# Chunk attention with two feed-forward layers: attention scores and values of a pair of heads as one operation each, from block 2 on

## The chip, the cores and the metric

The kernel runs on one core of one Trainium2 chip. The metric is the device time of one execution in microseconds, as the median over runs. Five engines work side by side and wait for one another by semaphores: TensorE (PE, with its weight loads as PEld), VectorE (DVE), ScalarE (ACT), GpSimd (POOL) and the queue of SyncE (SP) that issues transfers.

## The reference

Chunked attention with memory, then two feed-forward layers one behind the other on its output, all in float32. Inputs: q, k, v of 4 batches x 8 heads x 768 positions x 64; 8 memory keys and values for each head; weights 512x2048 and 2048x512 for each layer.

```
for c in range(nc):                          # chunks of 32 queries
    l_start = max(0, c_start - 16)
    r_end = min(S, c_end + 8)
    k_full = concat([mem_k, k[l_start:r_end]]);  v_full likewise
    scores = scale * q_c @ k_full.T
    a = softmax(scores)
    out[c_start:c_end] = a @ v_full
x = out as 3072 tokens x 512
x = (h * tanh(softplus(h))) @ w_out          # h = x @ w_in     (layer 1)
return (h * sigmoid(1.702 * h)) @ w2_out     # h = x @ w2_in    (layer 2)
```

## The kernel before

The 3072 tokens are cut into 8 blocks of 384 (`TB`), half a batch each. For a block the program does attention over all 8 heads, which leaves the block's activations split in a high and a low part (`xh`, `xl`, 128 x 4 x 384 each, one slice of 384 for each pair of heads), and then layer 1 in 16 steps of 128 hidden units (`step`): 12 matmuls of 128x384 into a bank `h` (line 904), the activation on ACT (916), a split in `gh` and `gl`, and 12 matmuls into the four output banks `o` (line 933). Each product is taken as three matmuls on the split parts. Layer 2 (lines 1066 and 1093) follows when all blocks are through layer 1.

The attention of block j runs in the gaps of layer 1 of block j-1. Blocks 0 and 1 (`EARLY`) are done in another way and stay as they are; from block 2 on a block has 4 pairs of heads, and each pair has two **quads**. A quad is 2 groups of 96 queries x 2 heads. `quad` (line 690) makes the scores of the quad: four f32 matmuls on 64 rows of the array (one head in rows 0-63, the other in rows 64-127), 96 queries against a window of 128 keys, head 0 into bank `s0`, head 1 into bank `s1`; each f32 matmul is two MATMUL instructions in the trace. Then DVE adds the mask and takes the minimum (722), ACT takes four exponentials (737), DVE divides (755 to 762). `quad_out` (line 780) turns the weights (791, four transposes into bank `s0`), copies them to `aT` (797/798), and multiplies with the values (817): two f32 matmuls with 128 columns of both heads' values against 192 columns of both heads' weights, into bank `s1`. Half of that product is of one head's values with the other head's weights and isn't used. The two useful quarters, 64x192 each, are copied to `xh` (843 on ACT or 845 on DVE) and their rests go to `xl` (849). `quads` calls `quad` for one quad and then `quad_out` for the quad before it.

Block 0's values (line 808) are done in yet another way: four matmuls with 64 columns of values, 96 columns of weights, head 0 into partitions 0-63 of the output, head 1 into 64-127.

The order of all work is made before the run by `Plan`: each operation is entered by `add` with a rank, its engines and a cost in microseconds; `issue` plays the engines through with these costs, lets each engine take the ready operation of lowest rank, and writes the instructions in the order of the starts. So on each engine the order is fixed, and the costs set only the order. Banks and buffers rotate by name (`Tag`): `s0` and `s1` have one bank each, `h` has two, `kT`, `qT` one buffer each, `e`, `aT`, `vt` two.

## Time and profile before

| what | value |
|---|---|
| median of 3 runs | 1202.54 us (1201.73 to 1203.37) |
| profiled execution, its own time | 1202.8 us |
| its span, first to last instruction | 1200.7 us |
| mean granted TensorE clock | 0.991 |
| TensorE busy (matmul) | 1181.3 us, 98% |
| VectorE busy | 820.0 us, 68% |
| ScalarE busy | 567.6 us, 47% |

Attention of block 0 fills the first 46 us. Layer 1 of the blocks 0 to 7 runs from there to 690 us, layer 2 from there to the end; the attention that the change touches (blocks 2 to 7) lies between 122 and 613 us. The chain that ended last goes through TensorE for 94% of the span. A row of a timeline merges neighbouring instructions of one kind: its start, the time to the end of the last of them, and their count. Matmuls are pipelined, so that one of 128x384 has a duration of 0.34 us and yet the next starts 0.17 us after it: what an operation costs TensorE is read from the starts of what stands behind it, not from its duration.

### The profile page before, as it was taken

To read this page: it belongs to the slowest core of one execution; us is meant where nothing else is said; L and a number is where in the kernel's file an instruction comes from. 1 tells how busy PE (TensorE), PEld (TensorE's weight loads), DVE (VectorE), ACT (ScalarE), POOL (GpSimd) and SP (SyncE) were. 2 spreads that over 40 slices of the span, in tenths; PEclk is the share of its full clock that TensorE was granted. 3 is DMA by queue.
4 is the path that set the end of the run, shared out by engine and by line. 5 is a ranking of instruction groups with operands and counts; after the bars stand their busy time and mean duration, and the time that the engine had idled before them with its cause. 6 is when DMAs were issued, how large, how long until landed. Compare 5 with 4: busy or idle time off the path is not lost.

```text
span 1200.7 us, 19141 instructions
## 1 busy us (share of the span) xinstructions
PE 1181.3 (98%) x6656; PEld 1081.9 (90%) x6656; DVE 820.0 (68%) x2373; ACT 567.6 (47%) x1324; POOL 10.0 (1%) x27
## 2 busy tenths in 40 slices
PE   7899999999999999999999999999999999999998
PEld 6677799999999999999999998898988898988897
DVE  5999877766776767667655677877756855555454
ACT  4887667666546565555523255435312521231112
POOL 1000000000000000000000000000000000000000
PEclk8899999999999999999999999999999999999999
DMA  9984554543333434434112767699756865566531
GB/s 203 259 279 158 151 142 130 131 97 92 101 91 92 112 81 111 99 85 106 54 44 71 254 219 237 220 365 308 237 185 212 290 218 193 193 231 202 180 107 53
DMA packets 214686, 197.79 MB, mean 165 GB/s; under 512 B 133496, under 2 KB 176519, under 8 KB 214591
## 3 DMA queue, kind: packets, MB, share of 16 engines
q1 hardware_dynamic: 214239, 195.82, 53.4%
q0 software_dynamic: 352, 0.75, 0.4%
q8 instruction: 53, 0.87, 0.3%
q14 instruction: 42, 0.34, 0.1%
HBM read 148.29 MB, written 48.23 MB: 164 GB/s over the span
## 4 chain that ended last, share of the span: by engine, by line
PE 94%; SPq 2%; DVE 1%; DMA 1%; ACT 1%; issue 0%; ACTq 0%
PE h L904 22%; PE o L933 22%; PE h L1066 20%; PE o L1093 15%; PE s L1093 7%; PE s L817 3%; PE s L709 3%; SPq L300 2%; PE s L791 1%; DMA vt<-in_v_dram 1%; DMA vt<-in_mem_v_dram 0%; ACT e L737 0%; ACT L737 0%; DVE wi L385 0%; ACT L916 0%
## 5 line engine op out<-in xcount | busy, mean ns | idle before, releaser
L904 PE MATMUL h<-xh,wi 128*128 128x384 f32 x1024 | 269.7, 344 | 2.1 <-ACT gl L916 1.2
L933 PE MATMUL o<-gh,wo 128*128 128x384 f32 x896 | 240.4, 349 | 0.0
L904 PEld LDWEIGHTS h<-xh,wi 128*128 128x128 f32 x1024 | 184.2, 189 | 10.5 <-ACT gl L916 1.6
L904 PE MATMUL h<-xl,wi 128*128 128x384 f32 x512 | 172.5, 337 | 0.0
L933 PEld LDWEIGHTS o<-gh,wo 128*128 128x128 f32 x896 | 158.1, 188 | 2.3
L933 PE MATMUL o<-gl,wo 128*128 128x384 f32 x448 | 150.7, 336 | 0.0
L916 ACT ACTIVATE u<-h 128x384 f32<-128x384 f32 x112 | 55.0, 491 | 137.0 <-PE h L904 128.6
L737 ACT ACTIVATE e<-e,mx 96x128 f32<-96x128 f32 x240 | 94.1, 393 | 27.8 <-DVE mx L722 27.2
L953 DVE TENSOR_TENSOR gl<-u,gh 128x384 fp32r<-128x384 f32 x177 | 97.2, 554 | 12.6 <-ACT gh L948 9.4
L904 PEld LDWEIGHTS h<-xl,wi 128*128 128x128 f32 x512 | 96.5, 188 | 0.0
L1066 PE MATMUL h<-wi,wi 128*128 128x384 f32 x480 | 94.7, 337 | 0.0
L1066 PEld LDWEIGHTS h<-wi,wi 128*128 128x128 f32 x480 | 85.6, 188 | 4.7
L1133 ACT ACTIVATE v<-h 128x384 f32<-128x384 f32 x61 | 30.0, 492 | 126.3 <-PE h L1066 126.2
L933 PEld LDWEIGHTS o<-gl,wo 128*128 128x128 f32 x448 | 84.1, 188 | 0.0
L1093 PE MATMUL o<-wo,gh 128*128 128x512 f32 x262 | 82.0, 394 | 0.0
L722 DVE CUSTOM_DVE_ANT_0 e<-s,mask 96x128 f32<-96x128 f32 x240 | 55.8, 283 | 34.6 <-PE s L709 33.3
L1066 PE MATMUL h<-wo,wi 128*128 128x384 f32 x384 | 76.9, 336 | 0.0
L1116 ACT ACTIVATE u<-e 128x384 f32<-128x384 f32 x64 | 33.4, 524 | 91.7 <-DVE e L1139 91.6
L916 ACT ACT_TABLE_LOAD x55 | 70.6, 1283 | 8.6 <-PE h L904 7.8
L737 ACT ACT_TABLE_LOAD x54 | 69.3, 1283 | 3.8 <-DVE mx L722 2.9
L1066 PEld LDWEIGHTS h<-wo,wi 128*128 128x128 f32 x384 | 68.3, 188 | 2.7
L845 DVE CAST xh<-s 64x192 fp32r<-64x192 f32 x86 | 30.5, 355 | 48.1 <-PE s L817 37.8
(199 smaller groups left out, 2058.8 us busy)
## 6 DMA issues: line engine op xcount, KB each, us to landing
wi<-w2c SPq DMA_DIRECT2D x72, 512.0 KB
wo<-w2o SPq DMA_DIRECT2D x48, 512.0 KB
w2c<-wi SPq DMA_DIRECT2D x24, 512.0 KB
st<-x1d SPq DMA_DIRECT2D x56, 192.0 KB
wi<-in_moe_w_in_dram SPq DMA_DIRECT2D x16, 512.0 KB
wo<-in_moe_w_out_dram SPq DMA_DIRECT2D x16, 512.0 KB
st<-in_moe_w_in_dram SPq DMA_DIRECT2D x16, 512.0 KB
w2d<-v SPq DMA_DIRECT2D x32, 256.0 KB
```

The costliest lines, as they stand in the source:

```text
L709: nc.tensor.matmul(out=s[hh][:, i, :], lhsT=queries(d, i), rhs=keys(d, i), start=True, stop=True,)
L722: nc.vector.tensor_tensor_reduce(out=e[:, i, hh, :], in0=s[hh][:, i, :], in1=mask[:GQ, mask_of(g0 + i), :], scale=-scale, scalar=-NEG, op0 ...
L737: nc.scalar.activation(out=e[:, i, hh, :], in_=e[:, i, hh, :], func=AF.Exp, scale=-1.0, bias=mx[:, i, hh:hh + 1], accum_out=sm[:, i, hh:hh ...
L817: nc.tensor.matmul(out=o[:, i].rearrange("p h t -> p (h t)"), lhsT=vt[:, g + i, h:h + 2].rearrange("p h d -> p (h d)"), rhs=aT[:, i].rearr ...
L845: nc.vector.tensor_copy(out=x, in_=y)
L904: nc.tensor.matmul(out=h.get(), lhsT=a[:, c], rhs=b[:, kk, :], start=(n == 0), stop=(n == 3 * KD - 1))
L916: add(i + 0.3, [("act", act(TB, True), lambda: nc.scalar.activation(out=u.get(), in_=h.get(), func=AF.Mish))], reads=[h], writes=[u], tabl ...
L933: nc.tensor.matmul(out=o.get(), lhsT=a[:, c], rhs=b.get(), start=(first and n == 0), stop=(last and n == len(prods) - 1),)
L953: add(rank + 0.05, [("dve", dve(TB), lambda: nc.vector.tensor_tensor(out=gl.get(), in0=u.get(), in1=gh.get(), op=ALU.subtract))], reads=[u ...
L1066: nc.tensor.matmul(out=bank.get(), lhsT=a, rhs=b, start=(fresh and m == 0), stop=(m == 3 * K2 - 1), skip_group_check=not fresh,)
L1093: nc.tensor.matmul(out=o.get(), lhsT=a[:, c], rhs=w[:, b:b + DM], start=(first and k == 0), stop=(last and k == 2))
L1116: add(rank, [("act", act(TB, True), lambda: nc.scalar.activation(out=u.get(), in_=src(), func=AF.Tanh, scale=0.851))], reads=[src.buf], wr ...
```

## The change

From block 2 on a pair of heads is one unit. `oct_scores` issues the scores of both quads in one operation, 8 matmuls of the same kind as before, into the whole banks `s0` (head 0, four groups) and `s1` (head 1). `quad` is called twice with these banks given and does the rest of the softmax for its half, the second with a rank 1.5 higher (`STAGGER`). `oct_out` turns the weights of each quad (the first into `s0`, the second into `s1`), copies them to `aT`, and then multiplies all values in one operation into `s1`: for each of 4 groups and each head one matmul with the head's 64 columns of values, in its half of the array's columns, against 96 columns of weights. The result is 128 x 384, all of it used, and goes to `xh` in one copy and to `xl` in one subtraction.

```diff
@@ -20,6 +20,7 @@
 WARM = 16
 LEAD = 8
 AHEAD = 6
+STAGGER = 1.5
 
 
 class Buf:
@@ -608,7 +609,7 @@
         return [
             (
                 lambda d, i, gp=gp: qT[d, (2 * gp + i) * GQ:(2 * gp + i + 1) * GQ],
-                lambda d, i, gp=gp: kT[d, 2 * gp + i, :],
+                lambda d, i, at=False, gp=gp: 2 * gp + i if at else kT[d, 2 * gp + i, :],
                 [qT, kT, whole],
             ) for gp in range(GB // 2)
         ]
@@ -687,16 +688,33 @@
             [qk],
         )
 
-    def quad(j, hp, gp, heads, rank):
+    def oct_scores(pair, rank):
+
+        s = [T[n].new([GQ, GB, P], F32) for n in ("s0", "s1")]
+
+        def scores():
+            for queries, keys, _ in pair:
+                for i in range(2):
+                    for hh in range(2):
+                        d = slice(hh * D, (hh + 1) * D)
+                        nc.tensor.matmul(
+                            out=s[hh][:, keys(d, i, True), :], lhsT=queries(d, i), rhs=keys(d, i), start=True, stop=True
+                        )
+
+        add(rank + 0.5, [("pe", 1.4, scores)], reads=pair[0][2], writes=s)
+        return s
+
+    def quad(j, hp, gp, heads, rank, given=None):
         b, s0 = divmod(j * TB, S)
         g0 = s0 // GQ + 2 * gp
         queries, keys, turned_from = heads
+        first = 2 * gp if given else 0
 
         names, after = ("s0", "s1"), ("s0", "s1")
         if j == 0:
 
             names, after = (names, ("o0", "o1"))[hp % 2], ("o2", "o3")
-        s = [T[n].new([GQ, 2, P], F32) for n in names]
+        s = given or [T[n].new([GQ, 2, P], F32) for n in names]
         e = T["ev" if j == 0 and hp % 2 else "e"].new([GQ, 2, 2, P], F32)
         mx, sm = T["mx"].new([GQ, 2, 2], F32), T["sm"].new([GQ, 2, 2], F32)
         r = T["r"].new([GQ, 2, 2, 1], F32)
@@ -714,14 +732,17 @@
                         stop=True,
                     )
 
-        add(rank + 0.5, [("pe", 0.87, scores)], reads=turned_from, writes=s)
+        if given:
+            after = (names[gp],) * 2
+        else:
+            add(rank + 0.5, [("pe", 0.87, scores)], reads=turned_from, writes=s)
 
 
         def least(hh):
             for i in range(2):
                 nc.vector.tensor_tensor_reduce(
                     out=e[:, i, hh, :],
-                    in0=s[hh][:, i, :],
+                    in0=s[hh][:, first + i, :],
                     in1=mask[:GQ, mask_of(g0 + i), :],
                     scale=-scale,
                     scalar=-NEG,
@@ -855,6 +876,58 @@
             )
             add(rank + 3.6, [("dve", dve(2 * GQ), lo)], reads=[o, part], writes=[x0[j][1]])
 
+    def oct_out(j, hp, vt, rank, es):
+
+        aTs = []
+        for n, e in enumerate(es):
+            t = T[f"s{n}"].new([P, 2, 2, GQ], F32)
+            aT = T["aT"].new([P, 2, 2, GQ], F32)
+
+            def turn(t=t, e=e):
+                for i in range(2):
+                    for hh in range(2):
+                        nc.tensor.transpose(t[:, i, hh, :], e[:, i, hh, :], ident[:GQ, :GQ])
+
+            r = rank + STAGGER * n
+            add(r + 2.2, [("pe", 0.33, turn)], reads=[e, ident], writes=[t])
+            add(
+                r + 2.4,
+                [
+                    ("act", act(TB, True), lambda t=t, aT=aT: nc.scalar.activation(
+                        out=aT.get(), in_=t.get(), func=AF.Copy)),
+                    ("dve", dve(TB), lambda t=t, aT=aT: nc.vector.tensor_copy(out=aT.get(), in_=t.get())),
+                ],
+                reads=[t], writes=[aT],
+            )
+            aTs.append(aT)
+        o = T["s1"].new([P, GB, GQ], F32)
+        h = 2 * hp % HV
+
+        def values():
+            for g in range(GB):
+                for hh in range(2):
+                    nc.tensor.matmul(
+                        out=o[hh * D:(hh + 1) * D, g], lhsT=vt[:, g, h + hh], rhs=aTs[g // 2][:, g % 2, hh],
+                        start=True, stop=True,
+                    )
+
+        add(r + 2.7, [("pe", 1.0, values)], reads=[vt, *aTs], writes=[o])
+        if j not in x0:
+            x0[j] = tuple(T[n].new([P, KD, TB], F32R) for n in ("xh", "xl"))
+        xh, xl = x0[j]
+        part = fixed()
+        flat = lambda: o.get().rearrange("p g t -> p (g t)")
+        add(
+            r + 2.9,
+            [
+                ("act", act(TB, True), lambda: nc.scalar.activation(out=xh[:, hp, :], in_=flat(), func=AF.Copy)),
+                ("dve", dve(TB), lambda: nc.vector.tensor_copy(out=xh[:, hp, :], in_=flat())),
+            ],
+            reads=[o], writes=[xh, part],
+        )
+        add(r + 3.1, [("dve", dve(TB), lambda: nc.vector.tensor_tensor(
+            out=xl[:, hp, :], in0=flat(), in1=xh[:, hp, :], op=ALU.subtract))], reads=[o, part], writes=[xl])
+
     def quads():
 
         last = None
@@ -876,14 +949,20 @@
                         pair = pair_of_heads(j, hp, rank)
                         if 2 * hp % HV == 0:
                             vals = values_of(j, 2 * hp // HV, rank)
-                    heads = pair[gp]
+                        s = oct_scores(pair, rank)
+                        oct_out(j, hp, vals, rank, [
+                            quad(j, hp, i, pair[i], rank + STAGGER * i, s)[1] for i in range(GB // 2)
+                        ])
+                    yield
+                    continue
                 now = (j, hp, gp, vals, rank, *quad(j, hp, gp, heads, rank))
                 if last:
                     quad_out(*last)
                 yield
                 last = now
-        quad_out(*last)
-        yield
+            if j == EARLY - 1:
+                quad_out(*last)
+                yield
 
 
     x1d = dram.tile([P, KD, NT], F32, name="x1d")
```

Two places of the order. First **TensorE**, between the values of one unit and the next scores, in a block late in layer 1 (`h` matmuls are the first, `o` matmuls the second product of a layer-1 step; `s` under `aT,vt` are values, `s` under `kT,qT` scores, `s` under `ident,e` transposes). Before, the transposes and values of a quad:

```order
L791 MATMUL s_5300<-ident,e 128x96 x4
L933 MATMUL o_4541<-gh,wo_2356 128x384 x2
L933 MATMUL o_4541<-gl,wo_2356 128x384
L933 MATMUL o_4549<-gh,wo_2356 128x384 x2
L933 MATMUL o_4549<-gl,wo_2356 128x384
L817 MATMUL s_5320<-aT,vt 128x192 x2
L933 MATMUL o_4558<-gh,wo_2356 128x384 x2
L933 MATMUL o_4558<-gl,wo_2356 128x384
L933 MATMUL o_4565<-gh,wo_2356 128x384 x2
L933 MATMUL o_4565<-gl,wo_2356 128x384
L904 MATMUL h<-xh,wi_579 128x384 x2
```

and further on, 30 large matmuls behind these values, the scores of the next quad but one, of which two of four are shown:

```order
L933 MATMUL o_4558<-gh,wo_2367 128x384 x2
L933 MATMUL o_4558<-gl,wo_2367 128x384
L933 MATMUL o_4565<-gh,wo_2367 128x384 x2
L933 MATMUL o_4565<-gl,wo_2367 128x384
L709 MATMUL s_5388<-kT,qT 96x128
L709 MATMUL s_5390<-kT,qT 96x128
```

Now, the values of a pair and behind them the scores of the next pair, of which two of eight are shown:

```order
L909 MATMUL s_5748<-aT,vt 64x96 x8
L1012 MATMUL o_5402<-gh,wo_1887 128x384 x2
L1012 MATMUL o_5402<-gl,wo_1887 128x384
L1012 MATMUL o_5407<-gh,wo_1887 128x384 x2
L1012 MATMUL o_5407<-gl,wo_1887 128x384
L1012 MATMUL o_5450<-gh,wo_1887 128x384 x2
L1012 MATMUL o_5450<-gl,wo_1887 128x384
L1012 MATMUL o_5462<-gh,wo_1887 128x384 x2
L1012 MATMUL o_5462<-gl,wo_1887 128x384
L700 MATMUL s_5780<-kT,qT 96x128
L700 MATMUL s_5782<-kT,qT 96x128
```

The values stand once for a pair instead of twice, as eight matmuls of 64x96 instead of four of 128x192 in two places, and the next scores are 12 large matmuls behind them here; before there were 30. Over the 23 places where a pair follows a pair the distance is now 12 (7 places), 14 or 15 (10), 18 (1) or 24 (5) large matmuls.

Second **ScalarE**, around the copy of the values' result into `xh` (`u<-h` is the layer-1 activation, `e,sm<-e,mx` are exponentials, each change between the two needs an ACT_TABLE_LOAD). Before, near the end of layer 1's attention:

```order
L916 ACT_TABLE_LOAD
L916 ACTIVATE u<-h 128x384 x2
L948 ACTIVATE gh<-u 128x384
L737 ACT_TABLE_LOAD
L737 ACTIVATE e,sm<-e,mx 96x128 x4
L843 ACTIVATE xh<-s_6816 64x192
L916 ACT_TABLE_LOAD
L916 ACTIVATE u<-h 128x384 x2
L737 ACT_TABLE_LOAD
L737 ACTIVATE e,sm<-e,mx 96x128 x4
L916 ACT_TABLE_LOAD
L916 ACTIVATE u<-h 128x384
```

Now, around the same pair of operations as in the TensorE piece:

```order
L995 ACTIVATE u<-h 128x384
L758 ACT_TABLE_LOAD
L758 ACTIVATE e,sm<-e,mx 96x128 x8
L995 ACT_TABLE_LOAD
L995 ACTIVATE u<-h 128x384
L345 ACTIVATE v<-st 128x512
L995 ACTIVATE u<-h 128x384
L896 ACTIVATE aT<-s_5721 128x384
L995 ACTIVATE u<-h 128x384
L923 ACTIVATE xh<-s_5748 128x384
L758 ACT_TABLE_LOAD
L758 ACTIVATE e,sm<-e,mx 96x128 x4
L995 ACT_TABLE_LOAD
```

Eight exponentials of a pair now mostly stand in one row, so that table loads fall from 111 to 77 in the program; the copy into `xh` stands behind an activation, a split or an `aT` copy in each of the 23 pairs in which ScalarE has it, never right behind exponentials. On **VectorE**, ahead of the next scores' minimum:

```order
L1032 TENSOR_TENSOR gl<-u,gh 128x384
L362 SCALAR_TENSOR_TENSOR v<-st,v 128x512
L1026 CAST gh<-u 128x384
L1032 TENSOR_TENSOR gl<-u,gh 128x384
L928 TENSOR_TENSOR xl<-s_5748,xh 128x384
L743 ISA e,mx<-s_5780,mask 96x128
```

The subtraction into `xl`, which frees bank `s1`, stands behind the split of a layer-1 step.

## Rows read from the trace of the kernel before

**Rows 1.** The page: busy time by engine, and the chain that ended last.

```profile
PE 1181.3 (98%) x6656; PEld 1081.9 (90%) x6656; DVE 820.0 (68%) x2373; ACT 567.6 (47%) x1324; POOL 10.0 (1%) x27
...
PE 94%; SPq 2%; DVE 1%; DMA 1%; ACT 1%; issue 0%; ACTq 0%
```

**Rows 2.** Windows of the span: length, busy us of each engine (instructions), granted clock, DMA share, GB/s.

```profile
122.00:208.00 86.00, 85.11 (x510) 76.42 (x509) 70.71 (x227) 58.39 (x132) 0.58 (x2) 1.00 0.55 145
...
290.00:371.00 81.00, 81.00 (x511) 77.57 (x510) 57.57 (x197) 47.89 (x109) 0.70 (x2) 1.00 0.40 102
...
613.00:690.00 77.00, 77.00 (x445) 77.00 (x444) 44.13 (x114) 22.57 (x55) 0.00 (x0) 1.00 0.40 138
690.00:1201.00 511.00, 507.00 (x2523) 455.52 (x2521) 318.39 (x723) 163.62 (x367) 0.00 (x0) 1.00 0.63 215
```

**Rows 3.** Waits of PE, 122 to 613 us: total us, times, longest.

```profile
PE h L904 <- DVE wi L385: 0.8, 1, 0.8
```

**Rows 4.** Timeline of PE around the scores of a quad: start, us, engine, line, count.

```profile
568.99 0.34 PE L933 MATMUL o<-gl,wo 128*128 128x384 f32 x1
569.26 0.68 PE L709 MATMUL s<-kT,qT 64*96 64x128 f32 x8
569.87 0.61 PE L904 MATMUL h<-xh,wi 128*128 128x384 f32 x2
570.32 0.34 PE L904 MATMUL h<-xl,wi 128*128 128x384 f32 x1
...
571.04 0.51 PE L904 MATMUL h<-xh,wi 128*128 128x384 f32 x2
...
571.56 0.51 PE L904 MATMUL h<-xh,wi 128*128 128x384 f32 x2
```

**Rows 5.** Timeline of PE around the values of a quad.

```profile
563.63 0.34 PE L933 MATMUL o<-gl,wo 128*128 128x384 f32 x1
563.81 0.81 PE L817 MATMUL s<-aT,vt 128*128 128x192 f32 x4
564.32 0.65 PE L933 MATMUL o<-gh,wo 128*128 128x384 f32 x2
564.81 0.33 PE L933 MATMUL o<-gl,wo 128*128 128x384 f32 x1
```

**Rows 6.** Timeline of PE cut at 569.6 us: the same scores, two instructions fewer.

```profile
569.26 0.57 PE L709 MATMUL s<-kT,qT 64*96 64x128 f32 x6
```

**Rows 7.** Timeline of PE in block 0's attention, values in column halves.

```profile
32.10 0.55 PE L808 MATMUL o<-aT,vt 128*64 128x96 f32 x8
32.58 0.30 PE L674 MATMUL h<-ident,wi 96*128 96x96 f32 x1
```

**Rows 8.** The same, cut at 32.11 us: its first two instructions.

```profile
32.10 0.30 PE L808 MATMUL o<-aT,vt 128*64 128x96 f32 x2
```

**Rows 9.** Windows: the clock there (columns as in Rows 2).

```profile
32.00:33.50 1.50, 1.50 (x22) 1.26 (x19) 1.50 (x8) 1.13 (x6) 0.00 (x0) 1.00 1.17 204
```

**Rows 10.** Instructions of line 808: duration ns min/median/max, first and last start.

```profile
L808 PEld LDWEIGHTS o<-aT,vt x64: 132/137/230, 20.2 to 40.2; 128*64 128x64 f32 x64
L808 PE MATMUL o<-aT,vt x64: 246/246/420, 20.2 to 40.4; 128*64 128x96 f32 x64
```

**Rows 11.** Instructions of line 817, its semaphore waits.

```profile
L817 PEldq EVENT_SEMAPHORE  x56: 51/51/767, 44.0 to 609.6; - x56
```

**Rows 12.** Groups of ACT, 122 to 613 us: count, busy us, mean ns, idle before.

```profile
L737 ACT ACTIVATE e<-e,mx 96x128 f32<-96x128 f32 x192 | 75.4, 394 | 27.1 <-DVE mx L722 26.5
L737 ACT ACT_TABLE_LOAD x48 | 61.6, 1283 | 3.7 <-DVE mx L722 2.9
...
L916 ACT ACTIVATE u<-h 128x384 f32<-128x384 f32 x94 | 46.1, 491 | 94.8 <-PE h L904 89.5 <-PE s L791 2.9 <-DMA kl<-in_k_dram 1.9
```

**Rows 13.** Groups of DVE, 690 to 1201 us: a subtraction or sum with a bank.

```profile
L1139 DVE TENSOR_TENSOR e<-e,h 128x384 f32<-128x384 f32 x64 | 35.4, 553 | 18.1 <-PE h L1066 15.8
```

**Rows 14.** Timeline of ACT: the copy of a quad's values into xh.

```profile
564.65 0.33 ACT L843 ACTIVATE xh<-s 64x192 fp32r<-64x192 f32 x1 [0.61 <-PE s L817]
```

## The prediction

> **What bounds the kernel now.** I read the page first: TensorE is busy 98% of the span and carries 94% of the chain that ended last [rows 1]. [...] Layer 1's last block and layer 2 behind it have TensorE busy 77 of 77 and 507 of 511 us. Third the waits: over 491 us TensorE itself waited 0.8 us for another engine [rows 3]. So in the touched stretch the time is what TensorE's instructions take one behind the other. A microsecond saved on TensorE is a microsecond of the kernel, as long as no other engine becomes late; VectorE and ScalarE have a quarter and two fifths of the time free, and what they save is worth nothing by itself.
>
> **What an attention operation costs TensorE now.** A busy time doesn't tell it, since matmuls overlap. I take the distance between the starts of the large matmuls around it and take off what these need alone. Alone, three large matmuls take 571.56 - 571.04 = 0.52 us [rows 4]. Around a quad's scores, from the large matmul ahead (568.99) to the third behind (570.32), it is 1.33 us, so the scores cost 1.33 - 0.52 = 0.81 us. Of this, their own stretch, first start to the first large start behind (569.26 to 569.87), is 0.61 us; the other 0.20 us is getting into the 64-row form and out of it. For a quad's values the same reading gives 564.81 - 563.63 - 0.52 = 0.66 us [rows 5]; they are in the array's full form and pay nothing for a change of form. The transposes stay as they are, four for each quad, and are left out.
>
> **Scores, eight matmuls in one operation.** Removed: one of two entries, exits and first instructions for each pair of heads. Added: nothing; the 16 instructions are those of two quads. What a further pair of instructions (both heads, side by side) costs is read by cutting the same stretch earlier: six instructions end 0.57 us after the first start, eight 0.68 us [rows 4, 6], so 0.11 us. Four further pairs are 0.44 us, and the operation costs 0.81 + 0.44 = 1.25 us where two cost 1.62. Saved: 0.37 us for each pair of heads.
>
> **Values, each head in its half of the columns.** Removed: eight instructions of 192 columns. Added: sixteen of 96 columns, which use half the array's columns. The same instruction stands in block 0's attention, and a piece of that ran at a clock of 1.00 as well [rows 9]. There eight instructions take 0.48 us from their first start to the next operation's [rows 7]. Two end at 0.30 us and eight at 0.55 us [rows 7, 8], so that a further pair, one of each head, costs 0.25 / 3 = 0.083 us: about 0.04 us an instruction. The two heads run side by side. Sixteen take 0.48 + 4 x 0.083 = 0.81 us. Entry and exit don't stand in block 0 between large matmuls; the nearest row is that of the scores, 0.20 us, and I take it. Bounds: 0 (as for the old values) and 0.4 us (twice the scores'). So 1.01 us in place of 2 x 0.66 = 1.32; saved 0.31 us, between 0.51 and 0.11.
>
> [...]
>
> **New waits in the values.** In half of the 24 pairs the values have just been loaded, and the order makes four of the eight matmuls wait for two transfers each. A wait instruction in front of a weight load took 51 ns in the old values [rows 11]. At most six of them fall inside the new operation: 12 x 6 x 0.051 = 3.7 us. TensorE's waits show none that the old ones cost [rows 3], since the sequencer is ahead of the array; I take 0 and keep 3.7 us for the upper end.
>
> **The split in one piece.** For each pair eight operations of 64x192 become one copy of 128x384 and one subtraction. That is work off ScalarE and VectorE, and so are 34 table loads of 1.28 us [rows 12]. TensorE covered all of it before; I cost it at nothing. But the way from the values over copy and subtraction to the next scores becomes shorter, because both banks stay taken through the whole pair. From the first start of the values: their end 0.55 + 4 x 0.083 = 0.88 us [rows 7, 8], the copy 0.03 us later (the old copy started at 564.65, its values ended at 563.81 + 0.81 = 564.62) [rows 5, 14], 0.49 us of copy as an activation of that size [rows 12], and 0.55 us of subtraction [rows 13]: 1.95 us. The next scores, at the closest twelve large matmuls behind, come at 0.81 + 0.20 + 12 x 0.174 = 3.10 us. There are 1.1 us to spare at 7 of 23 places, 1.5 to 1.7 at 10, 2.2 at one and 3.2 at five. A layer-1 split on VectorE ahead of the subtraction (0.55 us) still fits. I cost it at nothing.
>
> **The sum.** 24 pairs x (0.37 + 0.31) = 16.3 us. The profiled execution took 1202.8 us, so 1186.5; the median of the runs before lies 0.3 us under that execution, so 1186.2 us.
>
> **Rivals.**
> *The heads run one after the other.* If the column halves don't run side by side between large matmuls, a further instruction costs 0.083 us instead of a further pair: the sixteen take 0.81 + 8 x 0.083 = 1.47, with 0.20 us 1.67 us, 0.35 us more than before. 24 x (0.35 - 0.37) = -0.5 us: 1202.0, no change. Against it: [rows 7, 8] show them side by side in this very program; for it only that block 0's neighbours are small matmuls. Chance 0.03.
> *The bank comes back late (slower).* The copy into `xh` is on ScalarE in 23 pairs. If it stands behind a table load and four exponentials there, 1.28 + 4 x 0.39 = 2.84 us [rows 12], the next scores wait at 18 places: 7 x 1.74 + 10 x 1.24 + 0.6 = 25 us, so 1211. It decides from a lateness of 2.3 us (18 places eat 16 us), and from 2.5 us the kernel is slower by more than 0.2%. For it: the new chain is the only one that the change tightens, and one engine's order is fixed with costs that aren't the measured ones. Against it: the order never puts the copy right behind exponentials, and under the same planner TensorE waited 0.8 us in 491 [rows 3]. Chance 0.04; a mild form of it, with 6 to 14 us lost (1192 to 1200), 0.04.
> *No load overlaps.* Sixteen loads of 0.137 us [rows 10], each alone, and sixteen matmuls of 0.083 us make 3.5 us, with 0.20 us 3.7 us where 1.32 stood: +57 us, less 9 us of the scores: about 1251 us. Against it: eight such loads, 1.1 us in sum, lay inside a stretch of 0.48 us [rows 7, 10]. Chance 0.01. [...]
>
> **How the numbers follow.** The forecast has 0.88, the three rivals 0.03, 0.08 in both forms, and 0.01. About 0.2% (2.4 us) is what a measurement of this kernel can tell from no change. Faster: 0.88 + 0.04 = 0.92; the same 0.03; slower 0.04 + 0.01 = 0.05. The range: below, entry and exit of the values at half the price taken (24 x 0.1 = 2.4 us) and the 0.8 us of waiting gone, 1183; above, the semaphores' 3.7 us and twice 1 us for waits of the first pairs, which follow on block 1's other order, 1192. The bound of 0.4 us for entry and exit (1191) lies inside.
>
> **What would show it.** In the profile after: scores as runs of 16 instructions, 1.25 us by the same reading; values as runs of 16 of 128x96 with about 1.01 us; TensorE busy for all of a window in the touched stretch; the end of attention some 16 us earlier, near 597 instead of 613 us, and everything behind them shifted by the same amount with layer 2's length unchanged. Wrong steps would show as: values of 1.7 us or more (not side by side), gaps ahead of the scores put down to VectorE's subtraction (the bank), gaps inside the values behind a transfer's semaphore, or a layer 2 that is longer by what was saved. The prediction falls if any of these takes over 14 us in all.

## The result: 1185.6 us, 1.4% less than before

The changed kernel takes 1185.55 us in the median of four runs (1184.95 to 1186.28) against 1202.33 us for the kernel before in the same comparison, a ratio of 0.9861 with an interval of 0.9846 to 0.9875. That is 16.8 us less. The forecast was 1186.2 us, in a range of 1183 to 1192. The profiled execution took 1185.95 us, with a span of 1184.1 us.

The page of the changed kernel, its parts on the busy time by engine and on the chain that ended last; they answer to [rows 1]:

```profile
PE 1166.1 (98%) x6848; PEld 1068.0 (90%) x6848; DVE 758.6 (64%) x2218; ACT 530.4 (45%) x1306; POOL 9.1 (1%) x22
...
PE 95%; DVE 2%; ACT 1%; SPq 1%; DMA 1%; issue 0%; ACTq 0%
```

TensorE is still busy for 98% of the span and carries the chain. Its own time fell by 15.2 us, from 1181.3; VectorE's fell by 61 us (from 820.0) and ScalarE's by 37 us (from 567.6). Those two numbers are the larger ones, and they are not the gain.

Windows of the changed kernel (length, busy us of each engine with instructions, granted clock, DMA share, GB/s): a stretch in the middle of the touched part, layer 1's last block, layer 2; they answer to [rows 2]:

```profile
290.00:371.00 81.00, 81.00 (x560) 77.64 (x560) 48.43 (x175) 40.51 (x104) 0.00 (x0) 1.00 0.38 94
597.00:674.00 77.00, 77.00 (x444) 77.00 (x443) 43.21 (x111) 22.27 (x53) 0.00 (x0) 1.00 0.40 137
674.00:1184.10 510.10, 506.23 (x2519) 454.80 (x2517) 318.24 (x722) 163.16 (x367) 0.00 (x0) 1.00 0.63 215
```

In the touched part TensorE is busy for all of 81 us at a clock of 1.00 as before, while VectorE has 48.4 us of work there instead of 57.6. Layer 2's first matmul starts at 673.6 us instead of 690.3 in the trace of before, 16.7 us earlier; from that matmul to the end it is 510.5 us, before 510.4. So the whole gain lies in layer 1 and nothing is given back behind it.

A pair's scores in the timeline of TensorE, to be read as [rows 4]:

```profile
300.23 0.34 PE L983 MATMUL h<-xl,wi 128*128 128x384 f32 x1
300.50 1.12 PE L700 MATMUL s<-kT,qT 64*96 64x128 f32 x16
301.54 0.62 PE L1012 MATMUL o<-gh,wo 128*128 128x384 f32 x2
302.00 0.34 PE L1012 MATMUL o<-gl,wo 128*128 128x384 f32 x1
```

From the large matmul ahead (300.23) to the third behind (302.00) it is 1.77 us, less 0.52 us for three large matmuls: 1.25 us. The 24 operations have a median of 1.245 us, read in this way one by one, against 0.814 us for a quad before. A pair's values, to be read as [rows 5]:

```profile
316.36 0.34 PE L1012 MATMUL o<-gl,wo 128*128 128x384 f32 x1
316.63 0.88 PE L909 MATMUL s<-aT,vt 128*64 128x96 f32 x16
317.44 0.62 PE L1012 MATMUL o<-gh,wo 128*128 128x384 f32 x2
317.89 0.34 PE L1012 MATMUL o<-gl,wo 128*128 128x384 f32 x1
```

1.53 - 0.52 = 1.01 us; the median of the 24 is 1.013 us, against 0.656 us for a quad before. Sixteen instructions end 0.88 us after the first start, as added up from block 0's rows.

### The profile page after: what moved, and what is told of

Its sections match the earlier page's. It is cut to its first block, busy times and chain, and to the rows that moved or that the text cites. A ratio compares the mean times of both kernels' runs of the same rounds, so it can differ in the third digit from the quotient of the medians.

```text
span 1184.1 us, 19399 instructions
## 1 busy us (share of the span) xinstructions
PE 1166.1 (98%) x6848; PEld 1068.0 (90%) x6848; DVE 758.6 (64%) x2218; ACT 530.4 (45%) x1306; POOL 9.1 (1%) x22
## 3 DMA queue, kind: packets, MB, share of 16 engines
HBM read 148.29 MB, written 48.23 MB: 166 GB/s over the span
## 4 chain that ended last, share of the span: by engine, by line
PE 95%; DVE 2%; ACT 1%; SPq 1%; DMA 1%; issue 0%; ACTq 0%
PE o L1012 23%; PE h L983 22%; PE h L1145 20%; PE o L1172 15%; PE s L1172 8%; PE s L700 2%; PE s L909 2%; PE s L889 1%; SPq L301 1%; DMA wi<-in_q_dram 0%; PE s L727 0%; DMA vt<-in_mem_v_dram 0%; PE h L675 0%; PE o L829 0%; PE s L838 0%
## 5 line engine op out<-in xcount | busy, mean ns | idle before, releaser
L1012 PE MATMUL o<-gh,wo 128*128 128x384 f32 x896 | 235.7, 344 | 0.0
L995 ACT ACTIVATE u<-h 128x384 f32<-128x384 f32 x112 | 54.5, 490 | 163.4 <-PE h L983 129.0
L1026 DVE CAST gh<-u 128x384 fp32r<-128x384 f32 x140 | 48.8, 356 | 85.5 <-ACT u L995 84.6
L1145 PE MATMUL h<-wo,wi 128*128 128x384 f32 x384 | 76.9, 336 | 0.0
L1195 ACT ACTIVATE u<-e 128x384 f32<-128x384 f32 x64 | 33.4, 524 | 92.0 <-DVE e L1218 91.8
L743 DVE CUSTOM_DVE_ANT_0 e<-s,mask 96x128 f32<-96x128 f32 x240 | 54.3, 282 | 25.4 <-PE s L700 15.2
L1197 DVE SCALAR_TENSOR_TENSOR u<-u,h 128x384 f32<-128x384 f32 x32 | 17.7, 553 | 62.2 <-ACT u L1195 62.2
L1195 ACT ACTIVATE u<-h 128x384 f32<-128x384 f32 x32 | 15.7, 492 | 88.6 <-PE h L1145 88.6
```

The costliest lines, as they stand in the source:

```text
L743: nc.vector.tensor_tensor_reduce(out=e[:, i, hh, :], in0=s[hh][:, first + i, :], in1=mask[:GQ, mask_of(g0 + i), :], scale=-scale, scalar=-NEG,
L995: add(i + 0.3, [("act", act(TB, True), lambda: nc.scalar.activation(out=u.get(), in_=h.get(), func=AF.Mish))], reads=[h], writes=[u], tabl ...
L1012: nc.tensor.matmul(out=o.get(), lhsT=a[:, c], rhs=b.get(), start=(first and n == 0), stop=(last and n == len(prods) - 1),)
L1026: ("dve", dve(TB, True), lambda: nc.vector.tensor_copy(out=gh.get(), in_=u.get())),
L1145: nc.tensor.matmul(out=bank.get(), lhsT=a, rhs=b, start=(fresh and m == 0), stop=(m == 3 * K2 - 1), skip_group_check=not fresh,)
L1195: add(rank, [("act", act(TB, True), lambda: nc.scalar.activation(out=u.get(), in_=src(), func=AF.Tanh, scale=0.851))], reads=[src.buf], wr ...
```

## The experiments

All changes in this section are against the changed kernel or the kernel before, as said; a ratio is always against the kernel before on the same chip. The changed kernel itself was run a second time with two of them (1184.99 us).

The traces allow a finer comparison than the medians, though each holds one execution. Ahead of layer 1's 101st large matmul TensorE has 416 matmul instructions in each kernel of the table, and no edit touches them; yet that matmul starts at 72.9 to 76.9 us, and in two executions of the changed kernel at 75.93 and 75.42 us. From it to the end of the span these two take 1108.15 and 1108.13 us, and the clock stays at 1.00 up to 1180 us, in all but the last kernel of the table. In the table, us:

| kernel | start of the 101st | from there to the end | over the changed kernel |
|---|---|---|---|
| before | 75.38 | 1125.35 | 17.2 |
| changed | 75.93 | 1108.15 | |
| changed, second time | 75.42 | 1108.13 | 0.0 |
| the scores alone | 76.47 | 1115.96 | 7.8 |
| the column halves alone | 74.32 | 1126.65 | 18.5 |
| head by head | 76.86 | 1117.26 | 9.1 |
| two by two | 74.41 | 1109.12 | 1.0 |
| the split in four pieces | 72.94 | 1109.57 | 1.4 |
| a late bank, three subtractions | 74.79 | 1111.31 | 3.2 |
| a late bank, five subtractions | 73.87 | 1129.91 | 21.8 |

The last kernel of this section is left out, because it has other work ahead of that matmul.

### The scores alone

The scores of both quads in one operation as in the change; the values of each quad as before.

```diff
-        o = T["s1"].new([P, GB, GQ], F32)
+        for n, aT in enumerate(aTs):
+            o = T[f"s{n}"].new([P, 2, 2, GQ], F32)
...
-                for hh in range(2):
-                    nc.tensor.matmul(out=o[hh * D:(hh + 1) * D, g], lhsT=vt[:, g, h + hh], ...)
+                    nc.tensor.matmul(
+                        out=o[:, i].rearrange("p h t -> p (h t)"),
+                        lhsT=vt[:, 2 * n + i, h:h + 2].rearrange("p h d -> p (h d)"),
+                        rhs=aT[:, i].rearrange("p h t -> p (h t)"), start=True, stop=True)
```

> One part alone: scores of both quads in one operation as in the change, but the values of each quad as before (two 128x192 matmuls in the full form, split in four pieces). Theory (what an operation costs TensorE adds up; the scores save an entry, an exit and first instructions, 0.37 us a pair): 24 x 0.37 = 8.9 us under the kernel before, about 1193.5. Scores 1.25 us, values 0.66 us by the starts of the large matmuls around them. Rival (what cost was the unused half of the old values' product, the merged scores are worth little): no change, 1202.

Measured: 1194.09 us, ratio 0.9925 (0.9911 to 0.994), so 8.7 us under the kernel before, where 8.9 were expected. By the table it is 9.4 us under it. Its timeline of TensorE around a pair's scores:

```profile
304.21 0.34 PE L991 MATMUL h<-xl,wi 128*128 128x384 f32 x1
304.48 1.12 PE L700 MATMUL s<-kT,qT 64*96 64x128 f32 x16
305.52 0.62 PE L1020 MATMUL o<-gh,wo 128*128 128x384 f32 x2
305.99 0.34 PE L1020 MATMUL o<-gl,wo 128*128 128x384 f32 x1
```

1.78 - 0.52 = 1.26 us for the scores; the values of a quad, read in the same way, have a median of 0.655 us, as before. The merged scores are worth half of the gain by themselves.

### The column halves alone

Kernel before, with the values of a quad in column halves from block 2 on; the scores per quad as before.

```diff
-        apart = j == 0
+        apart = j == 0 or j >= EARLY
...
-        add(rank + 3.2, [("pe", 0.65, values)], reads=[vt, aT], writes=[o])
+        add(rank + 3.2, [("pe", 0.68 if j >= EARLY else 0.65, values)], reads=[vt, aT], writes=[o])
```

> The other part alone: scores per quad as before, values of each quad in column halves (four 64-column matmuls of 96, result 128x192 split in one piece). Theory: 0.48 us stretch + 0.20 us for entering and leaving the form = 0.68 us in place of 0.66, so 48 x 0.02 = +1 us, about 1203: halves alone gain nothing, they pay only when a pair's values share one entry. Rival (the unused half of the product was the cost): half of 0.66 us is saved 48 times, about 1187.

Measured: 1203.02 us, ratio 1.0004 (0.9995 to 1.0013): no change that the medians can tell; by the table 1.3 us more than the kernel before. A quad's values in its timeline:

```profile
307.70 0.34 PE L933 MATMUL o<-gl,wo 128*128 128x384 f32 x1
307.97 0.55 PE L808 MATMUL s<-aT,vt 128*64 128x96 f32 x8
308.45 0.62 PE L933 MATMUL o<-gh,wo 128*128 128x384 f32 x2
308.91 0.34 PE L933 MATMUL o<-gl,wo 128*128 128x384 f32 x1
```

1.21 - 0.52 = 0.69 us here, 0.683 us in the median, against 0.66 us for the old form [rows 5]; 48 times the difference of the medians is the 1.3 us of the table. 0.48 us is a stretch of their own, and 0.20 us lies outside it, as for the scores: no row of before showed this for column halves between large matmuls. The rival, that the unused half of the old product was the cost, would have put this kernel at 1187 us; it falls. But the half is not free either. The old four instructions start 0.162 us apart (at 563.806, 563.968, 564.130 and 564.292 us in the trace of [rows 5]), which accounts for 0.65 of their 0.66 us; the column halves need 0.083 us for each pair of instructions, 0.33 us for a quad. What takes this half back comes once for each operation: 0.683 us for four pairs and 1.013 us for eight leave 0.35 us for it, an estimate from these two lengths. So alone the halves gain nothing, and with one operation for a whole pair of heads they gain 24 x 0.3 us. The two parts alone give 9.4 us less and 1.3 us more by the table; together they give 17.2.

No run has a pair's values merged in the old form. By its starts nearly nothing of its 0.66 us comes once for each operation, so that a merge alone would have had next to nothing to save there; this is an estimate.

### Head by head

The changed kernel, the eight value matmuls in another sequence.

```diff
-            for g in range(GB):
-                for hh in range(2):
+            for hh in range(2):
+                for g in range(GB):
```

> The changed kernel with the eight value matmuls in another sequence: four of head 0, then four of head 1, so that neighbours are in the same half of the columns. Nothing else differs, the planned cost neither. Theory (neighbours in different halves run side by side, neighbours in the same half one after the other, 0.083 us each): the values cost 1.67 instead of 1.01 us, 24 x 0.66 = +16 us over the changed kernel, about 1201. Rival (an instruction of 96 columns by 64 takes 0.04 us whatever its neighbour): no change, 1185.5.

Measured: 1195.4 us, ratio 0.9937 (0.992 to 0.9953), 9.9 us over the changed kernel and 9.1 by the table. The sequence matters, but it costs 0.38 us a pair and not 0.66. The values in its timeline:

```profile
320.70 0.34 PE L1012 MATMUL o<-gl,wo 128*128 128x384 f32 x1
320.96 1.26 PE L909 MATMUL s<-aT,vt 128*64 128x96 f32 x16
322.16 0.62 PE L1012 MATMUL o<-gh,wo 128*128 128x384 f32 x2
322.61 0.34 PE L1012 MATMUL o<-gl,wo 128*128 128x384 f32 x1
```

1.91 - 0.52 = 1.39 us. That lies between the two expectations, so the theory "neighbours in the same half stand one after the other" was too simple. Cutting the stretch shows why. The first row below ends at 321.3 us, the second at 321.4:

```profile
320.96 0.54 PE L909 MATMUL s<-aT,vt 128*64 128x96 f32 x4
```

```profile
320.96 0.68 PE L909 MATMUL s<-aT,vt 128*64 128x96 f32 x6
```

By 321.3 us four instructions have started, all of head 0; by 321.4 two more, and one of these two is the first of head 1: single starts in the trace put the fifth of head 0 at 321.346 us and the first of head 1 at 321.352 (which of the two is which follows from the order of the program). So the second half began while three instructions of the first were still to come. If both halves run from there until head 0 has no more, there are 5 + 3 + 5 = 13 steps of 0.083 us (three of them shared) instead of 8, and the operation should cost 1.01 + 5 x 0.083 = 1.42 us, an estimate near the 1.39 measured.

### Two by two

This reading was tested with a sequence in which a head never has more than four instructions in a row.

```diff
-            for g in range(GB):
-                for hh in range(2):
-                    nc.tensor.matmul(...)
+            for n in range(2):
+                for hh in range(2):
+                    for g in (2 * n, 2 * n + 1):
+                        nc.tensor.matmul(...)
```

> The changed kernel with the value matmuls in blocks: two of head 0, two of head 1, and again. In the trace of the head-by-head kernel the array took the first instruction of head 1 when the fifth of eight of head 0 started, and then ran both. Theory (each half of the columns runs its own sequence, and up to three instructions can wait in front of a half while the other is served): four instructions of a head in a row never hold the other up, so 1.01 us as side by side, 1185.5 us. Rival (only direct neighbours run side by side, and that kernel's overlap came from its one turn in the middle): three of four instructions alone, about as long as head by head, 1195.

Measured: 1185.93 us, ratio 0.9865 (0.9848 to 0.9881), with the changed kernel at 1184.99 us (0.9855, 0.9841 to 0.987) beside it. The values:

```profile
315.24 0.34 PE L1013 MATMUL o<-gl,wo 128*128 128x384 f32 x1
315.51 0.93 PE L910 MATMUL s<-aT,vt 128*64 128x96 f32 x16
316.37 0.62 PE L1013 MATMUL o<-gh,wo 128*128 128x384 f32 x2
316.83 0.34 PE L1013 MATMUL o<-gl,wo 128*128 128x384 f32 x1
```

1.59 - 0.52 = 1.07 us (median of 24: 1.065), 0.05 us more than in strict alternation, and 1.0 us over the changed kernel by the table. The halves run side by side; in this operation the loss stands at the fifth instruction of one half, which starts 0.126 us behind the fourth instead of 0.083 (315.901 and 316.027 us). The rival would have given 1195. Instructions that wait in front of a half, as the expectation's theory has them, are not shown: both traces show starts alone, and the theory's 1.01 us was 0.05 us too low.

### The split in four pieces

The changed kernel, the result of the values copied and subtracted in four pieces of 64x192 as before, with the planner told so.

```diff
-            reads=[o], writes=[xh, part],
-        )
-        add(r + 3.1, [("dve", dve(TB), ...xl[:, hp, :]...)])
+        for n in range(2):
+            for hh in range(2):
+                ...
+                add(r + 2.9, [("act", act(2 * GQ, True), ...), ("dve", dve(2 * GQ), ...)], ...)
+                add(r + 3.1, [("dve", dve(2 * GQ), ...)], ...)
```

> The changed kernel with the result of the values split in four pieces of 64x192 again (four copies, four subtractions), so that VectorE and ScalarE have their old work back and the order is planned with it. Theory (TensorE alone bounds, the planner moves the next scores behind the longer split): within 1 us of the changed kernel, 1185.5. Rival (the split in one piece is part of the gain): 24 x up to 0.9 us of later scores, up to 1207.

Measured: 1185.04 us, ratio 0.9853 (0.9839 to 0.9868): the changed kernel's time in the median. By the table it takes 1.4 us more; that execution is early by 3 us at the 101st large matmul. The scores cost 1.7 us more in sum, 31.8 against 30.1, at places where the bank came later. VectorE has 787.7 us of work, 29 us more than in the changed kernel; ScalarE has no more than there (529.9 us), so its old work did not come back. "One split" is no part of the gain beyond 1.4 us.

### A late bank

The prediction's slower rival, the bank that comes back late, as a kernel: the subtraction that frees the bank is done three or five times, with the planned cost of one, so that the order stays as it is.

```diff
-        add(r + 3.1, [("dve", dve(TB), lambda: nc.vector.tensor_tensor(
-            out=xl[:, hp, :], in0=flat(), in1=xh[:, hp, :], op=ALU.subtract))], ...)
+        add(r + 3.1, [("dve", dve(TB), lambda: [nc.vector.tensor_tensor(
+            out=xl[:, hp, :], in0=flat(), in1=xh[:, hp, :], op=ALU.subtract) for _ in range(3)])], ...)
```

> The changed kernel with the subtraction that frees the bank done three times instead of once, each with the same result, and with the same planned cost, so that the order stays: the bank comes back about 1.0 us later (two subtractions of 0.55 us, started some 0.5 us apart). In the trace of the changed kernel the next scores start 0.9 to 1.0 us after the subtraction's end at 8 of 23 places, 1.6 us or more at the others. Theory (the slack is real, nothing else waits for the bank): 0 to 2 us over the changed kernel, 1185.5 to 1187.5. Rival (VectorE's later work matters, not the bank): 24 x 1.0 us, up to 1209.

> The same with five subtractions: the bank comes back some 2.1 us later. Theory: the scores wait 1.2 us at 8 places and 0.5 us at 9 with a slack of 1.6 us, 14 us over the changed kernel, about 1199.5. Rival (the bank is not what the scores wait for): no change, 1185.5; rival (VectorE's later work matters at every pair): 24 x 2.1 us, up to 1235.

First the changed kernel at a place with twelve large matmuls between values and scores: values on PE, copy on ACT, a layer-1 split and the subtraction on DVE, scores on PE (the window ends early, so the scores' count is cut):

```profile
492.58 0.88 PE L909 MATMUL s<-aT,vt 128*64 128x96 f32 x16
...
493.51 0.49 ACT L923 ACTIVATE xh<-s 128x384 fp32r<-128x384 f32 x1 [0.27 <-PE s L909]
...
493.74 0.56 DVE L1032 TENSOR_TENSOR gl<-u,gh 128x384 fp32r<-128x384 f32 x1
...
494.21 0.55 DVE L928 TENSOR_TENSOR xl<-s,xh 128x384 fp32r<-128x384 f32 x1
...
495.70 0.68 PE L700 MATMUL s<-kT,qT 64*96 64x128 f32 x8
```

The subtraction ends at 494.76 us and the scores start at 495.70: 0.94 us to spare. Over the 23 places this slack is 0.9 to 1.0 us at 8, 1.6 us at 8, 1.8 and 2.3 us at one each and 3.1 us at five.

With three subtractions 1188.61 us (ratio 0.9884, 0.987 to 0.9899), 3.1 us over the changed kernel; with five 1204.86 us (1.0018, 1.0008 to 1.0027), 19.3 us over it; by the table 3.2 and 21.8 us. Both are more than was expected. The place that answers to the one above, with five:

```profile
507.44 0.88 PE L909 MATMUL s<-aT,vt 128*64 128x96 f32 x16
...
508.37 0.49 ACT L923 ACTIVATE xh<-s 128x384 fp32r<-128x384 f32 x1 [0.27 <-PE s L909]
...
509.08 2.92 DVE L928 TENSOR_TENSOR xl<-s,xh 128x384 fp32r<-128x384 f32 x5
...
510.56 0.46 PE L700 MATMUL s<-kT,qT 64*96 64x128 f32 x2
...
512.14 1.08 PE L700 MATMUL s<-kT,qT 64*96 64x128 f32 x14 [1.13 <-DVE xl L928]
```

The scores' first two instructions, of head 0 in bank `s0`, start at their old place, 3.12 us behind the values; then TensorE stands until the last subtraction has ended (512.00) and goes on with the other fourteen. It is the bank `s1` that is waited for and nothing else, and the waits of TensorE say the same (total us, times, longest):

```profile
PE s L700 <- DVE xl L928: 12.9, 17, 1.5
```

The five subtractions took 2.92 us together, 0.59 us from one to the next and not 0.5 as the expectation had it. So the bank was 2.37 us late: 8 x (2.37 - 0.93) + 8 x (2.37 - 1.62) + 0.5 = 18 us. With three it was 1.18 us late, 8 x 0.25 = 2 us. By the starts around them, the 24 scores operations cost 20.3 us (with five) and 3.3 us (with three) more in sum than in the changed kernel, 50.5 and 33.4 against 30.1: with three that is all that was lost, at some 0.1 us more for each wait than the lateness alone. With five the rest of the 21.8 us, 1.4 us, goes with a lower clock: behind one of the longest waits, 1.5 us, TensorE ran for 3.4 us at a granted clock of 0.50. At that clock three large matmuls take 0.96 us instead of 0.52 (the changed kernel from 47.27 to 48.23 us), so that 3.4 us of it cost some 1.6 us, an estimate. The first window has the wait in it, the second is the one behind (columns as in the result's windows):

```profile
198.00:203.40 5.40, 3.88 (x30) 3.29 (x30) 4.18 (x10) 2.48 (x5) 0.00 (x0) 1.00 0.77 215
203.47:206.86 3.39, 3.39 (x13) 3.39 (x12) 3.39 (x19) 2.88 (x9) 0.00 (x0) 0.50 0.37 77
```

So the second rival of the five subtractions, that VectorE's later work costs at every pair, falls too: 24 x 2.37 us would be 57 us. The slack read from the rows of before, 1.1 us at the closest places, was 0.93 us.

### Block 1 in the same form

Since the cost of an operation was so regular, the changed kernel was extended to block 1: two neighbouring pairs of heads of the same two groups as one unit, four units.

```diff
+                    if j == 1:
+                        ...
+                        two = [turned(j, hp + m, st, rank + 0.1 * m) for m in range(2)]
+                        s = oct_scores_early(two, rank)
+                        oct_out(j, hp, st[2], rank, [
+                            quad(j, hp + m, gp, two[m], rank + STAGGER * m, s, m)[1] for m in range(2)
+                        ], gp)
```

> The changed kernel with block 1 in the same form: scores of two neighbouring pairs of heads of the same two groups in one operation, the values likewise in column halves, one split. Four such units. Theory: 4 x (0.37 + 0.31) = 2.7 us less on TensorE, about 1182.8 us. Rival: in the stretch where block 1's attention lies (46 to 122 us) VectorE is busy 71 of 76 us, and the longer way from scores to split makes TensorE wait there, so that 0 to 5 us are lost again: 1185 to 1190.

Measured: 1185.8 us, ratio 0.9866 (0.9851 to 0.9881), where 1182.8 was expected: 0.8 us over the changed kernel beside it. The saving is there in the operations: in layer 1 a unit's values cost 1.31 to 1.46 us, read as above, and the last unit's scores 1.40, while a quad of block 1 costs 0.80 to 1.10 us for its values and 0.96 to 1.26 for its scores in the changed kernel. What is lost is lost at the start. The trace is that of the slowest of the four executions (1187.28 us, the others 1185.6 to 1185.8), so how much of the following the others had is not shown. Windows of this kernel at the start of layer 1, then those of the changed kernel (columns as above):

```profile
46.00:54.00 8.00, 5.71 (x29) 4.92 (x26) 8.00 (x31) 5.11 (x14) 0.00 (x0) 0.50 1.11 320
54.00:62.00 8.00, 8.00 (x38) 7.43 (x37) 4.34 (x9) 4.51 (x12) 0.00 (x0) 0.81 0.85 295
```

```profile
46.00:54.00 8.00, 8.00 (x39) 6.98 (x38) 6.71 (x21) 6.62 (x12) 0.00 (x0) 0.77 1.14 278
54.00:62.00 8.00, 7.69 (x43) 5.81 (x42) 7.90 (x19) 5.86 (x15) 0.00 (x0) 1.00 1.05 364
```

In the first 8 us TensorE is busy for 5.7 us at a clock of 0.50, where the changed kernel has 8.0 us at 0.77. The planner puts the whole first unit of block 1 and the second unit's scores ahead of layer 1's first matmul. These scores wait 0.7 us for bank `s1`, until the first unit's subtraction has ended, and layer 1's first matmul waits for a bank too (total us, times, longest):

```profile
PE h L1022 <- ACT kT L682: 1.6, 1, 1.6
```

It writes to a bank `h` out of which ScalarE copies what was turned for a later unit only at 50.56 us. So it starts at 51.1 us instead of 46.0. Since more attention is done by then, most of this comes back: layer 1's 301st large matmul starts at 133.8 us instead of 132.7. The rival's range held, but not its way: what TensorE waits for are banks at the start of layer 1, and the clock stays at 0.50 up to 57.0 us, in the changed kernel up to 49.7.

## Why the prediction was right

**What bounds the kernel.** TensorE alone, in the touched stretch, where it was busy for all of a window before and is so now [rows 2]: right. VectorE and ScalarE got 61 and 37 us of work less, which shows nowhere in the time: the sum below closes without it. The split in four pieces, which gave VectorE 29 us back, cost 1.4 us. Table loads before exponentials fell from 48 to 31 in the touched stretch, and as many before layer-1 activations, as the order said; also without effect on the time:

```profile
L758 ACT ACT_TABLE_LOAD x31 | 39.8, 1283 | 16.5 <-DVE mx L743 16.1
```

**The scores, 1.25 us.** Measured 1.245; alone worth 8.7 us (9.4 by the table) where 8.9 were worked out.

**The values, 1.01 us.** Measured 1.013. The step that rested on the farthest row was the 0.20 us outside the operation's own stretch, taken from the scores and put down to entering and leaving the form; the column halves alone confirm the number (0.68 us for a quad, of which 0.20 us lies outside), not what it is spent on. That it fits to 0.01 us is in part luck: nothing before showed that column halves have as much outside their stretch as the 64-row form, and the bounds were 0 and 0.4 us. One reading behind it was wrong. The old values do not pay nothing by the same reading: their own stretch in [rows 5] is 564.32 - 563.81 = 0.51 us of 0.66, so that 0.15 us lies outside. By their starts that need not be the price of a form: the start of the large matmul behind is put 0.03 us after that of the fourth instruction, while the four start 0.16 us apart. So the stretches of two forms can't be compared with one another; the sum didn't do that.

**Weight loads.** The last rival had each of the sixteen loads stand alone, 3.7 us for the operation. The instructions of line 909 (duration ns min/median/max, first and last start):

```profile
L909 PEld LDWEIGHTS s<-aT,vt x384: 132/137/138, 142.5 to 592.8; 128*64 128x64 f32 x192
L909 PE MATMUL s<-aT,vt x384: 245/246/298, 142.5 to 592.8; 128*64 128x96 f32 x192
L909 PEldq EVENT_SEMAPHORE  x60: 51/51/836, 140.3 to 591.9; - x60
```

Sixteen loads of 137 ns are 2.2 us in sum and stand in an operation of 0.81 us from its first start to the next large matmul. So they overlap here, with both heads' loads on 128 rows (128*64 in the trace), and the rival falls. It is not a matter of the two column halves alone: the large matmuls, with 128 rows and 128 columns, start 0.17 us apart with loads of 0.19 us.

**Semaphores.** 60 wait instructions stand ahead of the values. In 12 of the 24 pairs the values have just been loaded; the 24 operations have costs from 1.005 us with a median of 1.013, and only the very first is longer (1.455 us, at 142 us; why is not shown). So in the other 23 these waits cost nothing, as taken. They are over ahead of the array: the 60 end 1.4 us in the median (0.1 to 2.8 us) before the next weight load of their line starts, and the 51 of line 817 between 122 and 613 us in the trace of before ended 2.1 us (0.04 to 3.2 us) before it.

**The way from the values to the next scores.** Estimated at 1.95 us with 1.1 us to spare; 2.0 to 2.3 us, once 2.6, and 0.9 to 1.0 us at the eight closest places measured. The late-bank kernels show that this new dependence could have turned the gain: 1.2 us of lateness cost 3 us, 2.4 us of lateness more than all of it. The prediction's break-even of 2.3 us was a little high: with the measured slacks and 0.1 us for each wait it is about 2.2 us, an estimate.

**The sum.** 16.3 us forecast, 16.8 measured. By the medians the operations save 48 x (0.814 + 0.656) - 24 x (1.245 + 1.013) = 16.4 us. By the table the gain is 17.2 us. The difference is TensorE's wait of 0.8 us for a weight split [rows 3], which isn't there any more in the touched stretch; the prediction had it in the lower end of its range and not in the sum.

## What to carry to other kernels

On an engine that is never idle, cost an operation by the starts of its neighbours, not by its busy time, and separate what comes once for each operation from what each further instruction costs, by two lengths of the same operation (here 0.683 and 1.013 us, which give 0.35 us for the one and 0.083 us for a pair of instructions for the other): the merge saved the first here, the narrower form the second, and the narrower form paid only because the merge came with it (alone it cost 1.3 us). To compare kernels more finely than their medians allow, take from a trace of each the time from the first instruction behind the part that varies to the end; here two executions of one kernel agree in it to 0.02 us. Where two halves of the array run side by side, issue their instructions alternately: here that took 1.01 us, head by head 1.39. When a merge holds a bank longer, measure the slack to the next user of that bank, since that is what can take the gain back: here 2.4 us of lateness cost 21.8 us.

## What the runs showed of the hardware

With head by head, the second half of the columns started 0.39 us after the first, while three instructions of the first half were still to come. Against strict alternation two matmuls of a head at a time cost 0.05 us more for sixteen instructions, four at a time 0.38 us. A subtraction with a duration of 0.55 us, repeated in place, starts every 0.59 us. And in the kernel with block 1's units TensorE was busy for 5.7 us of the 8 us from 46 to 54 us and its clock stood at 0.50 there, where the changed kernel had 8.0 us and 0.77. With five subtractions the clock stood at 0.50 from 203.5 to 206.9 us, behind a wait of TensorE of 1.5 us; the other 16 waits were not followed by this. The kernel with block 1's units was to save 2.7 us and has a median 0.8 us over the changed kernel's.
